# An attention and two-layer gated network kernel: the first unit's steps in another order, and the third unit's preparation later

## The chip, the cores and the metric

The kernel runs on one core of one Trainium2 chip. The metric is the device time of one execution in microseconds (us), from repeated runs; a profile is one more execution, with every instruction recorded.

## The reference, cut to what matters

Attention has two parts that are added: one over q, k, v averaged in groups of 4 positions (its result is repeated 4 times), and a local one in which a position sees those less than 4 away. Two gated layers of matrix products follow, over 2304 tokens of 512 features, with 2048 hidden features, all in float32.

```python
q_d = q.reshape(B, H, Sd, 4, D).mean(axis=3)          # k_d, v_d alike
out_up = np.repeat(sm_attn(q_d, k_d, v_d), 4, axis=2)
mask = np.abs(pos[:, None] - pos[None, :]) < 4
...
out = out_up + np.matmul(attn, v)                     # attn: softmax of the masked scores
h = x @ w_in;  x2 = (h * sigmoid(h)) @ w_out          # first layer (moe)
h = x2 @ w_in2; y = (h * clip(h + 3, 0, 6) / 6) @ w_out2   # second layer (moe2)
```

The four batches have 8 heads, 576 positions and 64 values per head; the inputs are drawn at random, and the weights come as 64-bit floats.

## The kernel before, in words

**Units and passes.** The 2304 tokens are cut into 8 units of 288 (half a batch); the work of a unit is its attention and then its first layer. The first layer runs over f = 0 to 15, slices of 128 hidden features. An iteration is one f of one unit: 12 matmuls `h<-xhl,w` (`gemm1`), the gate (`t` on ACT by a tanh, then on DVE), the split of the gated value into a high part `gh` (ACT) and a low part `gl` (POOL), and, up to two iterations later, 12 matmuls `y` (`y_unit1`). Every operand is split in a high and a low part, so that three products of the fast format make one of float32; `xhl` is such a pair of an input x. The order of the passes is: the first pass is unit 0 with f 0 to 7; the second is unit 1 with all 16; the third is unit 0 with f 8 to 15; then units 2 to 7 follow, and the second layer after them in blocks of 512 tokens.

**Weights.** The 32 weight tiles of a layer (`order` numbers them 0 to 31 as they are needed) are loaded as 64-bit words (`raw`, 512 KB each) and converted: ACT takes the upper words (`wu`), POOL or ACT the exponent bytes (`wt`), DVE joins them in two instructions (`wt<-wu,wt`), ACT rounds to the high part (`w<-wt`), and POOL subtracts for the low part (`w<-wt,w`). `step` does one such conversion; the first pass and the second have one or two steps in each iteration.

**The first unit's attention** stands in the list `PROLOGUE`, written out by hand. Its names: `turns` (k and q turned by matmuls `nt` with their sums), `ds` (averaged scores), `ls` (local scores), `sums` (v summed by fours on POOL: `vraw`, then `vd`), `dx` (maximum `dm` and exponential `de` of averaged scores), `dn` (normalized by `dr`), `dt` (transposed), `dv` (averaged values `od`), `le`, `ln`, `lt`, `lp` (local exponential, normalization, transposition to `leT`, and spreading into `pT`, a part of the tile `xo`), `lv` (local values, with `od` added: x of the unit), `warm` (n dummy matmuls `idle`), `keep_x` (x of unit 0 stored for the third pass). Every call is held behind what each engine was given last.

**Later units.** The attention of unit 1 is spread over the first pass, that of unit 2 over the second and third by `attention`: two places per iteration, 48 in all for unit 2. Before it comes the preparation: for each of 4 pairs of heads the loads of q and k into `qkraw` (a tile of two buffers, which `vraw` shares) and their transposes and sums on DVE (`xe<-qkraw`, `xe<-xe`, `xo<-xe`), then 8 loads and sums of v (`vd<-vraw`). In unit 2 they start at place 0, and the attention's steps at place 21.

**Order.** What is written is a program order; a scheduler then merges the engines' queues with regard to dependences and its own estimate of times, and may draw a load ahead where nothing holds it. Each engine, and SP's queue of loads, works strictly in the order of its own queue; a TensorE weight load may run ahead.

## Time and profile before

| | |
|---|---|
| median of 3 runs | 981.69 us (980.3 to 983.03) |
| the profiled execution | 980.93 us, of which 979.1 us lie between its first and last instruction |
| TensorE busy with matmuls | 944.3 us, 96% of the span |
| DVE, ACT, POOL busy | 46%, 40%, 26% of the span |
| mean granted clock of TensorE | 0.986 of full speed |

The time is read as a sum of stages: what TensorE does and where it waits. Busy shares over the whole span say little about the first 200 us, in which other engines have far more work than later.

### The profile page before, as it was taken

To read this page: it belongs to the slowest core of one execution; us is meant where nothing else is said; L and a number is where in the kernel's file an instruction comes from. 1 tells how busy PE (TensorE), PEld (TensorE's weight loads), DVE (VectorE), ACT (ScalarE), POOL (GpSimd) and SP (SyncE) were. 2 spreads that over 40 slices of the span, in tenths; PEclk is the share of its full clock that TensorE was granted. 3 is DMA by queue.
4 is the path that set the end of the run, shared out by engine and by line. 5 is a ranking of instruction groups with operands and counts; after the bars stand their busy time and mean duration, and the time that the engine had idled before them with its cause. 6 is when DMAs were issued, how large, how long until landed. Compare 5 with 4: busy or idle time off the path is not lost.

```text
span 979.1 us, 18978 instructions
## 1 busy us (share of the span) xinstructions
PE 944.3 (96%) x7654; PEld 829.4 (85%) x7654; DVE 448.4 (46%) x911; ACT 388.8 (40%) x894; POOL 257.9 (26%) x326
## 2 busy tenths in 40 slices
PE   8789797999999999999999999999999999999998
PEld 5677787999999989999999988888888888888897
DVE  4787588148361384432515878422223222322222
ACT  4576355324333342343425676333224222322232
POOL 6387484213222122132222688200000000000000
PEclk9789999999999999999999999999999999999999
DMA  7958722231231123101007960001002000100010
GB/s 188 328 122 247 210 59 36 75 65 41 69 63 23 49 49 69 39 7 52 2 1 255 370 218 1 1 22 65 0 1 74 13 1 1 43 1 1 1 44 22
DMA packets 125855, 71.68 MB, mean 73 GB/s; under 512 B 86088, under 2 KB 119112, under 8 KB 125768
## 3 DMA queue, kind: packets, MB, share of 16 engines
q1 hardware_dynamic: 121160, 65.76, 24.3%
q10 hardware_dynamic: 4608, 4.72, 1.4%
q8 instruction: 60, 0.98, 0.4%
q14 instruction: 27, 0.22, 0.1%
HBM read 59.83 MB, written 10.62 MB: 72 GB/s over the span
## 4 chain that ended last, share of the span: by engine, by line
PE 78%; DVE 8%; DMA 6%; SPq 2%; issue 2%; ACT 2%; POOL 1%; ACTq 0%; DVEq 0%; POOLq 0%
PE h L612 36%; PE y L749 21%; PE y L719 15%; DMA qkraw<-in_q_dram 2%; SPq L212 2%; DVE wt L31 2%; DMA x2raw<-x2d 2%; PE lv L203 1%; PE ls L203 1%; PE dv L203 1%; DMA xo<-in_v_dram 1%; DVE xe L31 1%; DVE le L31 1%; PE dt L206 1%; DMA nat<-in_q_dram 1%
## 5 line engine op out<-in xcount | busy, mean ns | idle before, releaser
L612 PE MATMUL h<-xhl,w 128*128 128x288 f32 (+2 forms) x2496 | 447.6, 327 | 9.5 <-DVE wt L31 4.5
L612 PEld LDWEIGHTS h<-xhl,w 128*128 128x128 f32 x2496 | 380.3, 189 | 50.6 <-ACT xhl L31 4.5
L719 PE MATMUL y<-gh,w 128*128 128x288 f32 x1024 | 233.0, 303 | 7.0 <-ACT w L31 5.1
L31 DVE SCALAR_TENSOR_TENSOR t<-t,h 128x288 f32<-128x288 f32 (+2 forms) x208 | 107.7, 519 | 273.8 <-ACT t L31 273.8
L749 PE MATMUL y<-w,g 128*128 128x512 f32 x864 | 214.8, 395 | 0.0
L749 PEld LDWEIGHTS y<-w,g 128*128 128x128 f32 x864 | 161.3, 188 | 37.5
L719 PEld LDWEIGHTS y<-gh,w 128*128 128x128 f32 x1024 | 172.8, 190 | 12.4 <-ACT w L31 5.4
L31 POOL TENSOR_TENSOR gl<-t,gh 128x288 fp32r<-128x288 f32 x112 | 90.9, 812 | 260.3 <-ACT gh L31 257.5
L719 PE MATMUL y<-gl,w 128*128 128x288 f32 x512 | 150.4, 302 | 1.8 <-DVE gl L31 1.4
L31 DVE TENSOR_TENSOR g<-t,g 128x512 fp32r<-128x512 f32 (+1 forms) x80 | 55.2, 689 | 124.4 <-ACT g L31 124.4
L31 ACT ACTIVATE t<-h,three 128x512 f32<-128x512 f32 (+1 forms) x80 | 51.7, 647 | 140.0 <-PE h L612 139.7
L719 PEld LDWEIGHTS y<-gl,w 128*128 128x128 f32 x512 | 97.2, 190 | 4.7 <-DVE gl L31 2.6
L31 POOL TENSOR_TENSOR w<-wt,w 128x512 fp32r<-128x512 f32 x64 | 84.1, 1318 | 46.4 <-ACT w L31 40.8
L31 DVE SCALAR_TENSOR_TENSOR wt<-wu,wt 128x512 uint32<-128x512 uint32 x128 | 85.6, 683 | 22.8 <-ACT wu L31 14.5
L31 ACT CAST gh<-t 128x288 fp32r<-128x288 f32 x128 | 55.0, 431 | 102.7 <-PE y L719 64.1
L31 ACT ACTIVATE t<-h 128x288 f32<-128x288 f32 x128 | 51.9, 407 | 107.1 <-PE h L612 104.5
L31 ACT CAST g<-t 128x512 fp32r<-128x512 f32 (+1 forms) x80 | 46.3, 579 | 119.5 <-PE y L749 118.8
L31 ACT CAST w<-wt 128x512 fp32r<-128x512 f32 x64 | 39.6, 620 | 28.6 <-DVE wt L31 24.2
L31 POOL TENSOR_SCALAR wt<-raw 128x512 uint32<-128x512 uint8 x61 | 42.2, 692 | 12.2 <-DMA raw<-in_moe_w_in_dram 5.8
L31 ACT ACTIVATE wu<-raw 128x512 f32<-128x512 f32 x64 | 40.2, 636 | 1.6 <-DVE t L31 0.9
L31 DVE STREAM_TRANSPOSE xe<-qkraw 128x288 f32<-128x288 f32 (+1 forms) x36 | 19.8, 566 | 27.3 <-DMA qkraw<-in_q_dram 12.0
L31 POOL TENSOR_TENSOR de<-de,dr 72x288 f32<-72x288 f32 x30 | 20.4, 683 | 34.0 <-DVE dr L31 27.9
(71 smaller groups left out, 572.9 us busy)
## 6 DMA issues: line engine op xcount, KB each, us to landing
raw<-in_moe_w_in_dram SPq DMA_DIRECT2D x32, 512.0 KB
raw<-in_moe_w_out_dram SPq DMA_DIRECT2D x32, 512.0 KB
xo<-in_v_dram SPq DMA_DIRECT2D x88, 64.0 KB
vraw<-in_v_dram SPq DMA_DIRECT2D x32, 144.0 KB
x2d<-yo ACTq DMA_DIRECT2D x32, 144.0 KB
x2raw<-x2d SPq DMA_DIRECT2D x9, 512.0 KB
out_dram<-yo SPq DMA_DIRECT2D x18, 256.0 KB
qkraw<-in_q_dram SPq DMA_DIRECT2D x96, 36.0 KB
```

The source lines that it names most:

```text
L31: r = getattr(self.engine, name)(*args, **kwargs)
L203: latest[0] = nc.tensor.matmul(*args, **kwargs).ins
L206: latest[0] = nc.tensor.transpose(*args).ins
L212: nc.sync.dma_start(raw[64 * h + 32 * e:64 * h + 32 * e + 32], src[h, t0:t0 + n, 32 * e:32 * e + 32].rearrange("(n t) d -> t n d", t=32),)
L612: nc.tensor.matmul(o, w[:, hw, c, :], x[:, hx, c, :], start=(i == 0), stop=(i == 3 * NC - 1))
L719: nc.tensor.matmul(ys[m], w[:, hw, m * P:(m + 1) * P], r, start=(f == fs[0] and i == 0), stop=(f == fs[-1] and i == 2),)
L749: nc.tensor.matmul(y, l[:, m * P:(m + 1) * P], w[:, hw, :], start=(f == 0 and i == 0), stop=(f == NF - 1 and i == 2),)
```

## The change

It does six things. (1) `ds` of both pairs of heads comes before the local scores, and the averaged softmax is done up to its transposes before the local one begins; its normalization is on POOL for all heads, the local subtraction on DVE for both halves. (2) The first weight tile is loaded ahead of v; the tiles 0 and 1 are converted and split inside the prologue (before, one conversion, one split and a second conversion stood ahead of `lv`), in the two halves `conv_parts` and `conv_join`; in the tiles 0, 7, 9, 11, 13 and 15 ACT does the bytes (before: the tiles 9, 12 and 17). (3) x of unit 0 is added from PSUM straight into its SBUF tile, and split from there by `split_x0`; before, it was added in PSUM and then both split and copied. (4) Of the four late query turns (q of unit 1), two stand in the prologue; their loads come after the weight tile 3 instead of after tile 9. (5) The three product groups of `gemm1` go hi-hi, lo-hi, hi-lo, where the low part of the weight came last. (6) In unit 2 the preparation starts at place 10 instead of 0 (its first load at place 9, held there by a memset, and each later load one step ahead of its use), and the attention's steps at place 25 instead of 21, in 20 places instead of 22.

```diff
@@ -163,20 +163,29 @@
+        conv_parts(layer, part, f)
+        conv_join(layer, part, f)
+    def conv_parts(layer, part, f):
         raw = raws[layer, part, f]
         words = raw.rearrange("p (d w) -> p d w", w=2)
         up = words[:, :, 1]
-        early = layer == 0 and order.index((part, f)) < 5
+        i = order.index((part, f)) if layer == 0 else NF
+        early = i < EARLY
         ps = (ps_y if early else ps_w).tile([P, 512], F32, tag="y" if early else "w", name="wu")
         act.activation(ps[:, :DM], up.bitcast(F32), AF.Copy, scale=2.0 ** -112)
         t = pool.tile([P, DM], U32, tag="wt", name="wt", bufs=3)
         b = raw.bitcast(U8).rearrange("p (d w) -> p d w", w=8)[:, :, 3]
-        if layer == 0 and not early and f < 8 and f % 4 == 3:
+        if i == 0 or EARLY < i < NF and i % 2:
             act.activation(t, b, AF.Copy, scale=2.0 ** -5, bias=-31.0 / 64)
         else:
             gps.tensor_scalar(out=t, in0=b, scalar1=2.0 ** -5, scalar2=-31.0 / 64, op0=ALU.mult, op1=ALU.add)
-        u = ps[:, :DM].bitcast(U32)
+        raws[layer, part, f] = t, ps[:, :DM].bitcast(U32)
+    def conv_join(layer, part, f):
+        t, u = raws[layer, part, f]
         vec.scalar_tensor_tensor(
             out=t, in0=u, scalar=0x80000000, in1=t, op0=ALU.bitwise_and, op1=ALU.bitwise_or
         )
@@ -224,6 +233,8 @@
     def load_qk(u, c):
         b, hf = divmod(u, 2)
         raw = pool.tile([P, (S + UT) // 32, 32], F32, tag="stg", name="qkraw", bufs=2)
+        if u == 2:
+            gps.memset(raw[:, 0:1, 0:1], 0.0)
         load_heads(raw[:, S // 32:], q[b, 2 * c:2 * c + 2], hf * UT, UT)
         if hf == 0:
             load_heads(raw[:, :S // 32], k[b, 2 * c:2 * c + 2], 0, S)
@@ -304,8 +315,9 @@
     def down_scores(u, ch):
         ss = []
+        own = u == 0 and ch == 1
         for par in range(2):
-            ps = ps_w.tile([P, 512], F32, tag="w", name="ds")
+            ps = (ps_y if own else ps_w).tile([P, 512], F32, tag="y" if own else "w", name="ds")
@@ -376,7 +388,7 @@
...
-        if u == 0:
+        if u == 0 and c == 1:
             keep_warm(idle["ps"], 1, latest[0], 448)
     def local_exp(eng, u, s):
...
-    def local_spread(par, t, a):
+    def local_spread(par, t, a, turning=False):
         rows = slice(32 * a, 32 * a + 32)
-        copy = act.copy if a % 2 else vec.tensor_copy
+        copy = act.copy if a % 2 or turning else vec.tensor_copy
         copy(pT[rows, par * NC * G:(par + 1) * NC * G, QB * a:QB * (a + 1)], t[rows, :, 0:QB])
     def local_values(u, g, od, x):
@@ -425,19 +437,21 @@
                     pT[:, (par * NC + c) * G + g, 0:n], start=True, stop=True,
                 )
         s = ps[:, :NC * n].rearrange("p (c t) -> p c t", c=NC)
-        o = s if u == 0 else x[:, :, g * n:(g + 1) * n]
+        o = x[:, :, g * n:(g + 1) * n]
         vec.tensor_tensor(
             out=o.rearrange("p c (i r) -> p c i r", r=FACTOR),
             in0=s.rearrange("p c (i r) -> p c i r", r=FACTOR),
             in1=od[:, :, g * nd:(g + 1) * nd].unsqueeze(3).to_broadcast([P, NC, nd, FACTOR]),
             op=ALU.add,
         )
-        if u == 0:
-            hi, lo = x[:, 0, :, g * n:(g + 1) * n], x[:, 1, :, g * n:(g + 1) * n]
-            act.copy(hi, s)
-            vec.tensor_tensor(out=lo, in0=s, in1=hi.bitcast(F32), op=ALU.subtract)
-            act.copy(xs[0][:, :, g * n:(g + 1) * n], s)
+    def split_x0(g):
+        n = 4 * QB
+        s = xs[0][:, :, g * n:(g + 1) * n]
+        hi, lo = (xhl[0][:, i, :, g * n:(g + 1) * n] for i in range(2))
+        act.copy(hi, s)
+        vec.tensor_tensor(out=lo, in0=s, in1=hi.bitcast(F32), op=ALU.subtract)
     xs = {}
     NPOS = 2 * NF
@@ -445,14 +459,14 @@
     def attention_calls(u):
         st = {}
-        local_engines = ((vec, gps), (gps, gps), (vec, vec))[min(u, 2)]
-        down_engines = (gps if u else vec, gps)
+        local_engines = ((vec, vec), (gps, gps), (vec, vec))[min(u, 2)]
+        down_engines = (gps, gps)
         def begin():
             st["od"] = pool.tile([P, NC, UD], F32, tag="od", name="od", bufs=1)
             if u == 0:
-                xhl[0] = st["x"] = pool.tile([P, 2, NC, UT], F32R, tag="xhl", name="xhl", bufs=1)
-                xs[0] = pool.tile([P, NC, UT], F32, tag="x32", name="x32", bufs=1)
+                xhl[0] = pool.tile([P, 2, NC, UT], F32R, tag="xhl", name="xhl", bufs=1)
+                xs[0] = st["x"] = pool.tile([P, NC, UT], F32, tag="x32", name="x32", bufs=1)
         def ds(ch): st["ds", 2 * ch], st["ds", 2 * ch + 1] = down_scores(u, ch)
         def dx(i): st["e", i] = down_exp(u, i, st["ds", i])
@@ -463,7 +477,7 @@
         def le(i): st["le", i] = local_exp(local_engines[i], u, st["ls"][i])
         def ln(i): local_norm(local_engines[i] if u else vec, st["le", i])
         def lt(i): st["leT", i] = local_transpose(u, st["le", i])
-        def lp(i, a): local_spread(i, st["leT", i], a)
+        def lp(i, a): local_spread(i, st["leT", i], a, u == 0 and i == 0)
         def lv(g):
             if u and g == 0:
                 xs[u] = st["x"] = pool.tile([P, NC, UT], F32, tag="x32", name="x32", bufs=1)
@@ -491,8 +505,14 @@
                     prep += [[(load_vd, (u // 2, h)), (prep_vd, (u // 2, h))]]
             else:
                 prep = [[(load_qk, (u, i)), (prep_q, (i,))] for i in range(NC)]
+            if u == 2:
+                loads = [calls[0] for calls in prep] + [None]
+                prep = [[loads[i + 1]] * (i + 1 < len(prep)) + calls[1:] for i, calls in enumerate(prep)]
+                places[9].append((held, loads[:1]))
+            start = 10 if u == 2 else 0
             for i, calls in enumerate(prep):
-                places[i * first // len(prep)].append((held, calls))
+                places[start + i * (first - start) // len(prep)].append((held, calls))
             for i in range(4 * G):
                 places[i * first // (4 * G)].append((load_vw, (u, i // 4, i % 4)))
         return places
@@ -530,14 +550,16 @@
         22: [("lv", 2)],
     }
+    EARLY = 5
     PROLOGUE = [
-        ("turns", 0), ("turns", 1), ("begin",), ("ds", 0), ("ls", 0), ("ls", 1), ("ls", 2), ("ls", 3), ("ds", 1), ("warm", 14), ("sums",),
-        ("dx", 0), ("dx", 1), ("le", 0), ("dx", 2), ("dx", 3), ("le", 1),
-        ("dn", 0), ("dt", 0), ("warm", 3), ("dn", 1), ("dt", 1), ("warm", 8), ("ln", 0), ("lt", 0), ("dv", 0),
-        ("dn", 2), ("dt", 2), ("warm", 3), ("dn", 3), ("dt", 3), ("warm", 8),
-        ("lp", 0, 0), ("lp", 0, 1), ("lp", 0, 2), ("lp", 0, 3), ("dv", 1), ("warm", 4), ("ln", 1), ("lt", 1),
-        ("lp", 1, 0), ("lp", 1, 1), ("lp", 1, 2), ("lp", 1, 3), ("step",), ("step",),
-        ("lv", 0), ("lv", 1), ("lv", 2), ("warm", 12), ("keep_x",), ("step",), ("step",), ("step",),
+        ("turns", 0), ("turns", 1), ("begin",), ("ds", 0), ("ds", 1), ("ls", 0), ("ls", 1), ("ls", 2), ("ls", 3),
+        ("sums", 0), ("dx", 0), ("dx", 1), ("parts", 0), ("dx", 2), ("dx", 3), ("dn", 0), ("dn", 1), ("join", 0),
+        ("warm", 10), ("dt", 0), ("dt", 1), ("sums", 1), ("le", 0), ("warm", 4), ("dv", 0), ("warm", 14), ("parts", 1), ("le", 1),
+        ("dn", 2), ("dn", 3), ("split", 0), ("dt", 2), ("dt", 3), ("warm", 5), ("dv", 1), ("warm", 20),
+        ("ln", 0), ("lt", 0), ("lp", 0, 0), ("lp", 0, 1), ("lp", 0, 2), ("lp", 0, 3),
+        ("ln", 1), ("lt", 1), ("lp", 1, 0), ("lp", 1, 1), ("lp", 1, 2), ("lp", 1, 3), ("join", 1),
+        ("lv", 0), ("lv", 1), ("lv", 2), ("xs", 0), ("split", 1), ("xs", 1), ("xs", 2), ("step",),
+        ("late", 0), ("late", 1), ("keep_x",), ("step",),
     ]
@@ -607,7 +629,7 @@
         w = wi[layer, f]
         o = hp[:, :n]
         i = 0
-        for hw, hx in ((0, 0), (0, 1), (1, 0)):
+        for hw, hx in ((0, 0), (1, 0), (0, 1)):
             for c in range(NC):
                 nc.tensor.matmul(o, w[:, hw, c, :], x[:, hx, c, :], start=(i == 0), stop=(i == 3 * NC - 1))
                 i += 1
@@ -668,20 +690,21 @@
         for j in range(2):
             kn[i, j] = load_nat(k, 0, 4 * i, j)
         qn[i] = load_nat(q, 0, 4 * i, 0)
+    load_w(0, *order[0])
     for h in range(H):
         load_vd(0, h)
     for i in range(4 * G):
         if i % 4 == 0:
-            load_w(0, *order[i // 4])
+            load_w(0, *order[1 + i // 4])
         load_vw(0, i // 4, i % 4)
-    for o in order[3:10]:
+    qn1 = [load_nat(q, 0, 4 * i, 1) for i in range(2)]
+    for o in order[4:10]:
         load_w(0, *o)
-    qn1 = [load_nat(q, 0, 4 * i, 1) for i in range(2)]
     for o in order[10:16]:
         load_w(0, *o)
     idle["ps"] = ps_y.tile([P, 512], F32, tag="y", name="idle")
     keep_warm(idle["ps"], 10)
-    add_w([(0, *o) for o in order])
+    add_w([(0, *o) for o in order[2:]])
     def turns(i):
         for c in (2 * i, 2 * i + 1):
@@ -693,15 +716,23 @@
     def warm(n):
         keep_warm(idle["ps"], n, latest[0], 224)
-    def sums():
-        for h in range(H):
+    def sums(i):
+        for h in range(4 * i, 4 * i + 4):
             prep_vd(0, h)
+    def late(c):
+        turn_q(c, qn1[c // 2])
+    def split(i):
+        split_w(0, *order[i])
+        done.add((0, *order[i]))
     names = attention_calls(0)
     def keep_x():
         nc.sync.dma_start(x0d, xs[0])
-    names.update(turns=turns, warm=warm, sums=sums, step=step, keep_x=keep_x)
+    names.update(turns=turns, warm=warm, sums=sums, step=step, keep_x=keep_x, late=late, split=split, xs=split_x0)
+    names.update(parts=lambda i: conv_parts(0, *order[i]), join=lambda i: conv_join(0, *order[i]))
     for name, *args in PROLOGUE:
         with behind(dict(last)):
             names[name](*args)
@@ -779,10 +810,10 @@
     HF = NF // 2
     passes = [(0, range(HF)), (1, range(NF)), (0, range(HF, NF))] + [(u, range(NF)) for u in range(2, NU)]
     first_att = attention(1, 2 * HF, lambda p: 1 + p * 12 // 22)
-    for c in range(NC):
+    for c in range(2, NC):
         first_att[0].insert(0, (late_q, (c, qn1[c // 2])))
     first_att[0].sort(key=lambda call: call[0] is not late_q)
-    second_att = attention(2, 3 * NF, lambda p: 21 + p)
+    second_att = attention(2, 3 * NF, lambda p: 25 + p * 20 // 22)
     nxts = [first_att, second_att[:2 * NF], second_att[2 * NF:]]
     nxts += [attention(u, NPOS, lambda p: 6 + p) for u in range(3, NU)] + [[[] for _ in range(NPOS)]]
     x0 = [None]
```

**DVE, first unit.** DVE's queue in the prologue, from the second averaged maximum on. Before:

```order
L31 TENSOR_REDUCE dm<-ds 72x2
L31 TENSOR_SCALAR dm<-dm 72x2
L31 TENSOR_TENSOR le<-ls,mask 128x384
L31 TENSOR_REDUCE lm<-le 128x12
L31 TENSOR_TENSOR le<-le,lm 128x384
L31 TENSOR_REDUCE dm<-ds 72x2
L31 TENSOR_SCALAR dm<-dm 72x2
L31 TENSOR_REDUCE dm<-ds 72x2
L31 TENSOR_SCALAR dm<-dm 72x2
L31 TENSOR_TENSOR le<-ls,mask 128x384
L31 TENSOR_REDUCE lm<-le 128x12
L31 TENSOR_SCALAR dr<-dr 72x2
```

After:

```order
L31 TENSOR_REDUCE dm<-ds 72x2
L31 TENSOR_SCALAR dm<-dm 72x2
L31 TENSOR_SCALAR dr<-dr 72x2
L31 RECIPROCAL dr<-dr 72x2
L31 TENSOR_SCALAR dr<-dr 72x2
L31 RECIPROCAL dr<-dr 72x2
L31 SCALAR_TENSOR_TENSOR wt<-wu,wt 128x512 x2
L31 TENSOR_TENSOR le<-ls,mask 128x384
L31 TENSOR_REDUCE lm<-le 128x12
L31 TENSOR_TENSOR le<-le,lm 128x384
L31 TENSOR_TENSOR le<-ls,mask 128x384
L31 TENSOR_REDUCE lm<-le 128x12
```

The first local half stood between the two pairs of averaged heads; now all averaged maxima and the first two sums `dr` stand ahead, with the join of weight tile 0, and the two local halves behind each other.

**PE, the first products.** PE's queue around the first `h` of the kernel (L612 before is L634 after, L203 is L212, L582 is L604, L719 is L750). Before:

```order
L582 MATMUL idle<-zeros 128x224
L612 MATMUL h<-xhl,w 128x288 x4
L203 MATMUL nt<-ident,nat 64x72 x13
L612 MATMUL h<-xhl,w 128x288 x8
L203 MATMUL nt<-ident,nat 64x72 x19
L719 MATMUL y<-gh,w 128x288 x4
L719 MATMUL y<-gl,w 128x288
```

After:

```order
L604 MATMUL idle<-zeros 128x224
L212 MATMUL lv<-xo 64x96 x3
L212 MATMUL nt<-ident,nat 64x72 x8
L212 MATMUL lv<-xo 64x96 x21
L212 MATMUL nt<-ident,nat 64x72 x8
L634 MATMUL h<-xhl,w 128x288 x8
L212 MATMUL nt<-ident,nat 64x72 x10
L634 MATMUL h<-xhl,w 128x288 x4
L212 MATMUL nt<-ident,nat 64x72 x6
L212 MATMUL ls<-xe 32x32 x86
L634 MATMUL h<-xhl,w 128x288 x12
```

Eight of the twelve products stand in one run now, since they need no low part of x; half of the late query turns `nt` lie ahead of them, and 12 dummy matmuls between `lv` and `h` are gone.

**DVE, second pass.** DVE's queue from the low parts of unit 1's x on. Before:

```order
L31 SCALAR_TENSOR_TENSOR wt<-wu,wt 128x512
L31 SCALAR_TENSOR_TENSOR t<-t,h 128x288 x2
L31 STREAM_TRANSPOSE xe<-qkraw 128x576
L31 STREAM_TRANSPOSE xe<-qkraw 128x288
L31 STREAM_TRANSPOSE xe<-qkraw 128x576
L31 STREAM_TRANSPOSE xe<-qkraw 128x288
L31 TENSOR_REDUCE xe<-xe 128x144
L31 TENSOR_REDUCE xo<-xe 128x72
L31 SCALAR_TENSOR_TENSOR wt<-wu,wt 128x512
L31 TENSOR_REDUCE xe<-xe 128x144
L31 TENSOR_REDUCE xo<-xe 128x72
L31 SCALAR_TENSOR_TENSOR t<-t,h 128x288 x2
```

After:

```order
L31 SCALAR_TENSOR_TENSOR wt<-wu,wt 128x512
L31 SCALAR_TENSOR_TENSOR t<-t,h 128x288 x2
L31 SCALAR_TENSOR_TENSOR wt<-wu,wt 128x512
L31 SCALAR_TENSOR_TENSOR t<-t,h 128x288
L31 SCALAR_TENSOR_TENSOR wt<-wu,wt 128x512 x2
L31 SCALAR_TENSOR_TENSOR t<-t,h 128x288
L31 SCALAR_TENSOR_TENSOR wt<-wu,wt 128x512 x2
L31 SCALAR_TENSOR_TENSOR t<-t,h 128x288
L31 SCALAR_TENSOR_TENSOR wt<-wu,wt 128x512 x3
L31 SCALAR_TENSOR_TENSOR t<-t,h 128x288
L31 SCALAR_TENSOR_TENSOR wt<-wu,wt 128x512 x2
L31 SCALAR_TENSOR_TENSOR t<-t,h 128x288
L31 STREAM_TRANSPOSE xe<-qkraw 128x288
```

Before, four transposes of unit 2 stand behind the gates `t` of the last iteration of the first pass and the first of the second, and ahead of three joins; now the first stands behind the gate of the sixth iteration.

## Rows read from the trace of the kernel before

**Rows 1.** Busy time by stage (PE, PEld, DVE, ACT, POOL), then clock, DMA share, GB/s

```profile
43.30:89.80 46.50, 42.53 (x544) 37.86 (x545) 35.49 (x76) 34.32 (x82) 37.41 (x53) 0.89 0.74 205
89.80:167.40 77.60, 63.30 (x607) 59.00 (x605) 62.36 (x123) 38.47 (x94) 44.81 (x52) 0.96 0.50 117
167.40:198.70 31.30, 31.30 (x284) 29.69 (x283) 7.12 (x18) 11.99 (x34) 7.70 (x11) 1.00 0.23 60
198.70:979.10 780.40, 773.62 (x5661) 678.48 (x5660) 318.38 (x637) 283.13 (x636) 145.16 (x165) 1.00 0.18 52
```

**Rows 2.** Chain of waits: start, length (us), what

```profile
259.47 3.19 PE y L719 x24
```

**Rows 3.** Timeline of all engines, first unit: start, length, engine, line, operation, [wait]

```profile
12.15 1.42 POOL L31 TENSOR_TENSOR vraw<-vraw 72x256 f32<-72x256 f32 x2 [3.59 <-DMA vraw<-in_v_dram]
...
29.44 1.35 POOL L31 TENSOR_TENSOR de<-de,dr 72x288 f32<-72x288 f32 x2 [3.60 <-DVE dr L31]
```

**Rows 4.** The same, end of the first unit's averaged values, added x, first gate

```profile
34.41 0.28 ACT L31 COPY od<-dv 128x144 f32<-128x144 f32 x1 [0.99 <-PE dv L203]
...
39.01 0.56 DVE L31 TENSOR_TENSOR lv<-lv,od 128x384 f32<-128x384 f32 x1
...
48.18 0.41 ACT L31 ACTIVATE t<-h 128x288 f32<-128x288 f32 x1 [0.56 <-PE h L612]
```

**Rows 5.** Timeline of PE around the first products

```profile
35.62 2.19 PE L203 MATMUL lv<-xo 128*64 128x96 f32 x42 [0.16 <-ACT xo L31]
...
43.28 0.79 PE L612 MATMUL h<-xhl,w 128*128 128x288 f32 x4 [4.20 <-ACT xhl L31]
...
45.85 2.29 PE L612 MATMUL h<-xhl,w 128*128 128x288 f32 x8
```

**Rows 6.** Groups of instructions, whole run: busy us, mean ns of one, waits before

```profile
L31 POOL TENSOR_SCALAR wt<-raw 128x512 uint32<-128x512 uint8 x61 | 42.2, 692 | 12.2 <-DMA raw<-in_moe_w_in_dram 5.8 <-DMA x2d<-yo 1.4
...
L31 ACT COPY xo<-leT 32x288 f32<-32x288 f32 x32 | 13.7, 430 | 7.9 <-DVE dr L31 4.1 <-DVE leT L31 3.4
...
L31 POOL TENSOR_TENSOR vd<-vraw 72x128 f32<-72x128 f32 x8 | 3.4, 452 | 0.0
...
L31 ACT ACTIVATE wt<-raw 128x512 uint32<-128x512 uint8 x3 | 2.0, 669 | 0.0
```

**Rows 7.** Stretch of 10 to 15 us, columns as in rows 1

```profile
10.00:15.00 5.00, 4.93 (x111) 3.91 (x114) 3.42 (x9) 4.33 (x8) 2.36 (x4) 1.00 0.90 244
```

**Rows 8.** Groups of DVE from 89.8 to 167.4 us, columns as in rows 6

```profile
L31 DVE SCALAR_TENSOR_TENSOR wt<-wu,wt 128x512 uint32<-128x512 uint32 x32 | 21.5, 679 | 2.0 <-POOL wt L31 1.8
L31 DVE TENSOR_REDUCE vd<-vraw 72x128 f32<-72x512 f32 x8 | 8.6, 1089 | 0.7 <-DMA vraw<-in_v_dram 0.7
L31 DVE SCALAR_TENSOR_TENSOR t<-t,h 128x288 f32<-128x288 f32 x17 | 7.4, 440 | 0.6 <-ACT t L31 0.6
...
L31 DVE STREAM_TRANSPOSE xe<-qkraw 128x288 f32<-128x288 f32 x8 | 3.7, 460 | 10.6 <-DMA qkraw<-in_q_dram 10.6
...
L31 DVE STREAM_TRANSPOSE xe<-qkraw 128x576 f32<-128x576 f32 x4 | 3.0, 762 | 1.2 <-DMA qkraw<-in_k_dram 1.2
...
L31 DVE TENSOR_TENSOR le<-le,lr 128x384 f32<-128x384 f32 x2 | 2.4, 1250 | 0.0
```

**Rows 9.** Timeline of DVE in the second pass

```profile
110.42 0.48 DVE L31 STREAM_TRANSPOSE xe<-qkraw 128x288 f32<-128x288 f32 x1 [8.59 <-DMA qkraw<-in_q_dram]
```

**Rows 10.** Timeline of PE: two waits of the second pass

```profile
101.94 0.51 PE L719 MATMUL y<-gh,w 128*128 128x288 f32 x1 [5.13 <-ACT w L31]
...
160.26 3.25 PE L612 MATMUL h<-xhl,w 128*128 128x288 f32 x12 [2.05 <-DVE wt L31]
```

**Rows 11.** Stretches behind these two waits, columns as in rows 1

```profile
103.00:105.00 2.00, 2.00 (x10) 1.87 (x9) 0.00 (x0) 0.60 (x3) 0.25 (x1) 0.50 1.06 376
...
160.00:164.00 4.00, 3.74 (x17) 3.75 (x18) 3.96 (x12) 1.81 (x5) 2.89 (x4) 0.57 0.00 0
```

**Rows 12.** Chain of waits: a load of unit 2's preparation

```profile
113.22 3.29 DMA qkraw<-in_k_dram
```

## The prediction, made before the changed kernel was run

> **What bounds the kernel now.** I read the busy time by stage first. From 198.7 us on TensorE (PE) works 773.6 of 780.4 us, nothing of the change lies there, and so all that can be won or lost lies ahead of it [rows 1]. In the three passes before, the reader should compare each engine with the length. In the third pass PE is busy for the whole 31.3 us. In the first pass it is busy 42.5 of 46.5 us, and no other engine is near the length. In the second pass it works 63.3 of 77.6 us, part of that at the lower clock, while DVE works 62.4: there the two hinder each other. An iteration (12 `h` and 12 `y`) needs about 3.19 us of PE, by the 24 products of one link in the chain of waits [rows 2], so the 24 iterations of second and third pass need 76.6 us, and they take 108.9.
>
> Then the timeline of the first 50 us: PE begins its first `h` at 43.28, after 4.20 us of waiting for the high part of x, and only at 48.18 the first gate starts [rows 4, 5]. What stands ahead is a chain: v arrives, POOL sums it from 12.15 on, and normalizes the last exponentials `de` until 30.79 [rows 3]; ACT has `od` at 34.69 [rows 4].
>
> Last the second pass by DVE's groups and its timeline: it idles 15.2 us, of which 10.6 and 1.2 are waits for the loads of q and k [rows 8], 8.59 in one place [rows 9]. Weight joins `wt` stand behind these in DVE's queue, and PE waits 5.13 us for a weight [rows 10].
>
> **The change, part by part.** *First unit.* The first weight's load, now ahead of v, is 0.5 MB; at the 244 GB/s of that stretch [rows 7] it delays v by 2.1 us, and POOL starts at 14.3. Its new queue is four heads at 0.71 + 0.45 us (4.6 us, to 18.9), two `de` (1.35, to 20.3), four heads (to 24.9), one `wt` of 0.69 (to 25.6), two `de` (to 27.0) [rows 3, 6]. With 0.5 us for waits between (my choice) that is 27.5. Before, `od` was there 3.9 us after this point (34.69 − 30.79) [rows 3, 4]; with and without two of ACT's spreading copies of 0.43 us [rows 6] in between that makes 30.5 to 31.4, and I take 31.0. All of the first half's spreading is now ACT's: six copies, 2.6 us, to 33.6. The local values start at about 34.0, or at 35 if the 20 dummies ahead run at 1.2 GHz. The 48 `lv` with 8 late turns between them take 2.5 + 0.6 us by the 2.19 us of 42 [rows 5], to 37.1. The last addition of 0.56 us [rows 4] and a rounding of nearly the same size on ACT bring the first `h` to 38.2 instead of 43.28. The additions no longer wait for each other's split, since they go to SBUF. Eight `h` (0.79 for four [rows 5]) need no low part of x, four more follow behind ten turns; ACT has three `wu`, two `xe` and one `w` ahead of the gate, some 3.9 us, so the gate starts at 42.1 instead of 48.2. **Gain 6.0**, from 4.5 (dummies at the low clock, more waits) to 7.5 (no waits, ACT's queue shorter).
>
> *First pass.* Two of four late turns are already done, and ACT does the bytes of three more tiles, 0.67 us each, which POOL is spared (0.69 each) [rows 6]. ACT then has about 34.3 + 2.0 less two turns' copies, POOL 37.4 − 2.1, in 46.5 us [rows 1]: neither becomes the bound, but neither was the only one either, since the conversions of two tiles per iteration pass in turn through ACT, POOL, DVE and ACT. I take the length as **unchanged**, ±2.
>
> *Second pass.* Unit 2's preparation leaves the first five iterations. There DVE has only two joins (0.68 each) and a gate (0.44) [rows 8], 1.8 us in an iteration of 3.2: it idles 1.4 us in each, over six iterations 8 us, but PE is never kept waiting. At the end some 5 us of DVE's attention work, such as the two normalizations of 1.25 us [rows 8] with their transposes and copies, falls behind the pass. The loads are now held until place 9, behind all weight loads; in before the last of k took 3.29 us with little beside it [rows 12]. Each is issued one step ahead of its use, so I set 2.5 us of waits for all four pairs, between nothing and the 8.59 of one wait [rows 9]. DVE's pass then lasts 62.4 − 5 + 8 + 2.5 = 67.9 instead of 77.6 us: **gain 9.7**, bounds 12 (no waits) and 4 (the 5 us stay, or a wait as long as now).
>
> A stretch of this pass gets denser, though. From f = 5 to 12 DVE has 17 joins (11.5 us), 8 gates (3.5), the transposes of four pairs (4.8), as much again (an estimate) for their reductions, and 8 sums of v (8.6) [rows 8]: 33 us in eight iterations, 4.1 each, where PE needs 3.2. PE then waits about 0.9 us in every iteration. What its clock does there is open. Behind the wait of 5.13 us the granted clock was 0.50, the 1.2 GHz level, and around the one of 2.05 it was 0.57 [rows 10, 11], where 12 products took 3.25 us against half of 3.19 [rows 2]. No row shows waits of under 1 us one behind the other lowering it, so I put nothing into the sum. The Trainium skill ("TensorE: Matmul & The Clock Gate", section "HAM oscillation — how this bites in real kernels") speaks against this change: it says that gaps that come back in every turn of a loop keep returning the clock to its low level, each burst starting cold. By the rule the dense stretch would go at the low clock again and again, which is the third rival below; the two rows agree as to single long waits.
>
> *Third pass.* Unit 2's attention starts two iterations later and ends one later, at place 45 of 48. Between its last values and its first `h` the addition (0.56), four roundings and four subtractions must fit into the last iteration's rest and two groups of `y` (about 1.6 + 3.2 us) [rows 2, 4]. DVE is busy 7.1 of 31.3 us here, ACT 12.0 [rows 1], so the 5 us from above and this are nearly covered; PE would show what isn't. **Loss 1.5**, from 0 to 3.
>
> *Product order.* The same 12 products; no cost. The low part of w, now needed four products earlier, is done by POOL well ahead except in f = 0.
>
> Sum: 6.0 + 0 + 9.7 − 1.5 = 14.2 us. The profiled execution took 980.93 us, 0.76 below the median of 981.69. So the profile would show about 966.7, and the median 967.5. A difference of 0.3% (2.9 us) is about what a measurement can tell from none.
>
> **The rivals.**
> 1. *Both gains, as worked out*: 967.5, by the bounds of the terms 958 to 973. For it: the waits of both places are seen in the profile. Chance 0.62.
> 2. *The first unit's gain is given back in the first pass*, because conversions set its pace and not the start of the products: weight tiles arrive no earlier (the loads run at 244 GB/s already at 10 to 15 us [rows 7]) and their conversion on ACT and POOL begins when the prologue releases them. Against it: ACT and POOL idle 12.2 and 9.1 of 46.5 us [rows 1]. 981.69 − 9.7 + 1.5 = 973.5. Chance 0.12.
> 3. *PE's clock falls in the dense stretch.* At 1.2 GHz an iteration takes 6.4 us instead of DVE's 4.1; if four of the eight run so, that costs 4 × 2.3 = 9 us: 976.5. Against it: waits of 0.9 us are less than the 2.05 after which it was seen. Chance 0.11.
> 4. *2 and 3 together*: 982.5, no difference. Also here if the preparation's waits eat what the first unit gives. Chance 0.06.
> 5. *Slower: DVE is blocked by the later loads.* Each pair's loads are now issued only when a buffer and its memset on POOL come free, and DVE's queue has joins behind each transpose. If each of four pairs waits as the one of 8.59 us does now [rows 9], the pass takes 62.4 − 5 + 8 + 34.4 = 99.8, 22 more than now: 981.69 − 6.0 + 22.2 + 1.5 = 999.5. It decides when all these waits exceed 2.5 + 14.2 = 16.7 us, two such waits. Against it: the long wait fell into a stretch where weights were still loading, and the load of k later took 3.29 [rows 12]. Chance 0.09.
>
> **How the numbers follow.** The likeliest case gives 967.5. To hold 8 in 10, the range takes in the first three cases, from 957 to 977. The first three are faster (0.85 in all), the fourth is within 0.3%, 0.06, and the last slower, 0.09.
>
> **What would show it.** In the changed kernel's timeline: the first `h` near 38 and the first gate near 42 us; POOL's last `de` of the first unit by 27.5. If the first pass still ends near 89.8 although it began 6 earlier, rival 2 holds; it should end near 84. In the second pass PE no longer waits some 5 us for a `w` near its start, DVE waits less than 2 us for any `qkraw`, and the granted clock between f = 5 and 12 stays above 0.9; a value near 0.6 is rival 3, waits of 8 us for `qkraw` are rival 5. The third pass should begin at 151 to 153 and unit 2's products at about 184 to 185, with PE waiting under 3 us for x there. Later rows should not move but by this shift. The prediction would be wrong above all if an engine that I take as covered, ACT in the prologue or POOL with its memsets, turns out to stand ahead of a join.

## The result, and the profile after

The change took the median from 982.36 to 972.12 us (4 runs each; those of the changed kernel lie between 969.37 and 973.22). A fourth run of the kernel before, 985.68, is why its median is no longer 981.69. The ratio is 0.9888, with a 95% interval of 0.9852 to 0.9925: faster. The gain is 10.2 us where 14.2 were forecast, and the time lies in the range of 957 to 977, 4.6 above the 967.5. The profiled execution took 973.22 us, 971.4 of them between first and last instruction, 7.7 less than before. Where they came from is read from the busy time by stage of the changed kernel, cut at the first `h` of each pass (columns as in [rows 1]):

```profile
43.92:90.39 46.47, 39.57 (x504) 35.51 (x504) 38.25 (x78) 33.41 (x81) 34.69 (x50) 0.85 0.60 175
90.39:157.26 66.87, 60.39 (x597) 56.17 (x597) 52.34 (x93) 34.37 (x78) 46.78 (x57) 1.00 0.57 144
157.26:191.84 34.58, 34.31 (x299) 31.35 (x297) 15.89 (x49) 16.61 (x53) 9.74 (x12) 1.00 0.37 80
191.84:971.40 779.56, 772.09 (x5662) 678.16 (x5660) 318.35 (x637) 282.99 (x636) 145.71 (x165) 1.00 0.18 52
```

Cut in the same way, the kernel before has its first `h` at 43.28, the second pass at 89.83, the third at 167.38 and unit 2 at 198.66. So the first unit lost 0.6 us where the forecast had it win 5.1 at the first `h` (and 6.0 at the first gate); the first pass kept its length (46.5 and 46.5); the second became 10.7 shorter (66.9 against 77.6, 67.9 forecast) and the third 3.3 longer (34.6 against 31.3); the rest gained 0.9. That sums to 7.7.

The first unit is where forecast and profile part. The timeline of the changed kernel, engine by engine (start, length, then the wait in brackets):

```profile
5.04 0.72 PE L212 MATMUL nt<-ident,nat 72*64 72x72 f32 x16
6.38 0.72 PE L212 MATMUL nt<-ident,nat 72*64 72x72 f32 x16 [0.62 <-DMA nat<-in_k_dram]
8.00 1.23 PE L212 MATMUL nt<-ident,nat 72*64 72x72 f32 x16 [0.90 <-DMA nat<-in_q_dram]
...
9.65 3.15 PE L212 MATMUL nt<-ident,nat 72*64 72x72 f32 x48
...
14.83 1.42 POOL L31 TENSOR_TENSOR vraw<-vraw 72x256 f32<-72x256 f32 x2 [6.00 <-DMA vraw<-in_v_dram]
...
25.68 1.29 POOL L31 TENSOR_TENSOR de<-de,dr 72x288 f32<-72x288 f32 x2 [5.73 <-DVE dr L31]
...
43.92 1.33 PE L634 MATMUL h<-xhl,w 128*128 128x288 f32 x8 [0.79 <-ACT xhl L31]
...
48.63 0.40 ACT L31 ACTIVATE t<-h 128x288 f32<-128x288 f32 x1
```

and its windows there (columns as above):

```profile
6.00:8.00 2.00, 0.72 (x16) 0.57 (x16) 0.61 (x2) 1.14 (x2) 1.68 (x6) 0.96 1.08 240
8.00:26.00 18.00, 18.00 (x337) 14.21 (x340) 7.83 (x24) 10.36 (x27) 5.54 (x12) 0.50 0.90 212
```

v is summed from 14.83 on, near the forecast 14.3, and the two `de` were expected at 18.9; but POOL waits 5.73 us for their `dr`, since the averaged scores are late. They are late because PE waited 0.62 and 0.90 us for loads of k and q, and then ran from 8 to 26 us at a granted clock of 0.50, the 1.2 GHz level: 48 turns take 3.15 us. In the kernel before the first 48 turns run in one piece, the window from 6 to 8 us has PE at work for 1.99 of 2.00 us, and the clock stays up (48 turns take 1.72 us):

```profile
5.57 2.38 PE L203 MATMUL nt<-ident,nat 72*64 72x72 f32 x48
7.88 0.36 PE L582 MATMUL idle<-zeros 128*128 128x448 bf16 x1
8.17 1.72 PE L203 MATMUL nt<-ident,nat 72*64 72x72 f32 x48
```

```profile
6.00:8.00 2.00, 1.99 (x47) 1.74 (x43) 0.46 (x1) 1.22 (x3) 1.68 (x6) 1.00 0.83 211
8.00:20.00 12.00, 9.64 (x303) 7.52 (x302) 6.97 (x15) 7.73 (x18) 7.33 (x14) 1.00 0.87 213
```

### The profile page after: what moved, and what is told of

Same layout as the page of the kernel before. It is cut to its first block, busy times and chain, and to the rows that moved or that the text cites. A ratio compares the mean times of both kernels' runs of the same rounds, so it can differ in the third digit from the quotient of the medians.

```text
span 971.4 us, 18968 instructions
## 1 busy us (share of the span) xinstructions
PE 944.6 (97%) x7652; PEld 830.7 (86%) x7652; DVE 447.9 (46%) x908; ACT 389.2 (40%) x896; POOL 259.6 (27%) x328
## 4 chain that ended last, share of the span: by engine, by line
PE 80%; DVE 7%; DMA 4%; issue 2%; POOL 2%; ACT 2%; SPq 2%; ACTq 0%; DVEq 0%; POOLq 0%
PE h L634 36%; PE y L780 21%; PE y L750 16%; DMA x2raw<-x2d 2%; SPq L221 2%; PE lv L212 2%; DVE wt L31 1%; PE dv L212 1%; PE ls L212 1%; PE nt L212 1%; PE ds L212 1%; POOL w L31 1%; DVE dm L31 1%; DVE le L31 1%; POOL wt L31 1%
## 5 line engine op out<-in xcount | busy, mean ns | idle before, releaser
L634 PE MATMUL h<-xhl,w 128*128 128x288 f32 (+2 forms) x2496 | 448.3, 328 | 7.8 <-DVE t L31 3.1
L634 PEld LDWEIGHTS h<-xhl,w 128*128 128x128 f32 x2496 | 380.9, 189 | 49.3 <-DVE t L31 3.8
L750 PE MATMUL y<-gh,w 128*128 128x288 f32 x1024 | 230.9, 301 | 3.4 <-ACT gh L31 2.2
L750 PEld LDWEIGHTS y<-gh,w 128*128 128x128 f32 x1024 | 171.1, 189 | 8.9 <-ACT gh L31 3.1
L750 PE MATMUL y<-gl,w 128*128 128x288 f32 x512 | 150.4, 301 | 1.7 <-DVE gl L31 1.6
L750 PEld LDWEIGHTS y<-gl,w 128*128 128x128 f32 x512 | 96.9, 189 | 4.6 <-DVE gl L31 2.6
L31 POOL TENSOR_TENSOR de<-de,dr 72x288 f32<-72x288 f32 x32 | 22.4, 703 | 35.8 <-DVE dr L31 24.0
L31 DVE TENSOR_REDUCE vd<-vraw 72x128 f32<-72x512 f32 x24 | 25.4, 1075 | 8.8 <-DMA vraw<-in_v_dram 4.2
```

Source lines behind the costliest of these rows:

```text
L31: r = getattr(self.engine, name)(*args, **kwargs)
L634: nc.tensor.matmul(o, w[:, hw, c, :], x[:, hx, c, :], start=(i == 0), stop=(i == 3 * NC - 1))
L750: nc.tensor.matmul(ys[m], w[:, hw, m * P:(m + 1) * P], r, start=(f == fs[0] and i == 0), stop=(f == fs[-1] and i == 2),)
```

## The experiments

Theory at first: the weight's load, now ahead of v, delays k and q and so lowers the clock. Rivals: chance in one execution; or the clock is not what holds the first unit. Apart from this the runs try whether the third unit's later work alone gives the gain of the passes. The runs after the first two of the table were made in three groups (a_again to u2_late_only, fill to steps_23, before_fill to steps_27); each group has its own runs of the kernel before (medians 982.0 to 983.0), so that a ratio to those is safer than a difference of two medians from different groups. The stages in the one profile of each run (us; "waits" is what DVE waits for `qkraw` and `vraw` from 100 to 170 us), and the median of its runs:

| run | first `h` | first pass | second | third | waits | median (runs) |
|---|---|---|---|---|---|---|
| before | 43.28 | 46.55 | 77.55 | 31.28 | 12.5 | 982.36 (4) |
| after | 43.92 | 46.47 | 66.87 | 34.58 | 2.6 | 972.12 (4) |
| a_again | 43.81 | 46.43 | 69.58 | 34.61 | 4.2 | 969.46 (6) |
| w0_behind_v | 44.27 | 46.70 | 64.67 | 34.60 | 1.8 | 966.65 (6) |
| u2_as_before | 37.86 | 46.79 | 76.78 | 31.23 | 9.9 | 974.07 (7) |
| u2_late_only | 45.74 | 48.12 | 65.49 | 34.82 | 2.8 | 976.39 (12) |
| fill | 38.53 | 46.19 | 69.76 | 34.62 | 4.2 | 966.88 (5) |
| fill_w0_behind_v | 36.84 | 46.14 | 64.32 | 34.60 | 1.1 | 965.21 (5) |
| few_dummies | 43.36 | 46.25 | 64.32 | 34.60 | 1.7 | 969.49 (5) |
| steps_23 | 36.97 | 45.81 | 73.99 | 33.32 | 2.4 | 974.74 (9) |
| before_fill | 42.34 | 49.57 | 78.01 | 31.24 | 12.8 | 980.39 (12) |
| fill_old_products | 38.38 | 46.65 | 69.62 | 34.82 | 4.7 | 971.59 (6) |
| fill_late_as_before | 36.69 | 50.50 | 67.74 | 34.61 | 3.2 | 968.72 (6) |
| steps_27 | 39.02 | 45.92 | 66.24 | 34.72 | 2.7 | 968.28 (6) |

**a_again**, the changed kernel unaltered. 

> The changed kernel once more. Theory (the first weight's load, ahead of v, delays the loads of k and q, PE waits between its first turns, and its clock falls to 0.50 from 8 us on): the fall stands in this profile too, the granted clock of 10 to 20 us is about 0.50, the first h starts at 43 to 44 us, time 970 to 973 us. Rival (the fall was chance in one execution): clock 1.00 there, first h at about 38, time 966 to 968.

 The profile shows the fall again (first `h` at 43.81), but its execution took 975.06, the longest of six that begin at 967.77. So the fall is no accident of one execution, and yet the median, 969.46, lies between the two cases. A mean granted clock is on record for every execution: a fall from 8 to 26 us should lower it by about 18.00 × 0.5 / 971, or 0.009. Of the ten executions of the changed kernel five have 0.979 to 0.981 (969.77 to 975.06 us, median 973.2), both profiles among them, and five 0.985 to 0.989 (967.77 to 971.03, median 969.2). So about half of them seem to have the fall.

**w0_behind_v**

```diff
-    load_w(0, *order[0])
     for h in range(H):
         load_vd(0, h)
+    load_w(0, *order[0])
```

> The changed kernel with the first weight tile's load behind the eight loads of v, as it stood before; PE's queue is the same. Theory (load delays k and q): the 48 turns run in one piece, the clock of 10 to 20 us is 1.00, the averaged scores are done at 15 instead of 21 us, the first h starts at 37 to 39, and the time falls by about 5 to 966 to 968 us. Rival 1 (the clock falls for another reason, such as the order of the turns): clock 0.50 there, first h at 43 to 44, 970 to 973. Rival 2 (conversions set the first pass): first h at 38, but the second pass still begins at about 90, and the time stays at 970 to 973.

 The clock fell all the same (0.53 from 8 to 26 us), after PE had waited 0.20 and 0.80 us. The load's place is not the cause of the fall, and the first theory is dead.

```profile
6.38 0.72 PE L212 MATMUL nt<-ident,nat 72*64 72x72 f32 x16 [0.20 <-DMA nat<-in_k_dram]
7.90 0.72 PE L212 MATMUL nt<-ident,nat 72*64 72x72 f32 x16 [0.80 <-DMA nat<-in_q_dram]
```

```profile
8.00:26.00 18.00, 18.00 (x375) 14.32 (x376) 8.51 (x25) 10.83 (x28) 6.25 (x13) 0.53 0.96 221
```

The median is nevertheless 966.65. The profile is of the slowest of the six executions, 971.56: it and one more (970.24) have a mean clock of 0.980, the other four 0.989 to 0.991 and 964.90 to 967.26 us. The median is one of executions that seem not to have the fall.

**u2_as_before**: in the changed kernel, places 10 and 25 back to 0 and 21.

```diff
-            gps.memset(raw[:, 0:1, 0:1], 0.0)
...
-    second_att = attention(2, 3 * NF, lambda p: 25 + p * 20 // 22)
+    second_att = attention(2, 3 * NF, lambda p: 21 + p)
```

> The changed kernel with the third unit's preparation and attention at their old places (no memset, loads from place 0, steps from place 21). Theory (this part alone gives the gain, 10.7 us in the second pass less 3.3 in the third): the second pass lasts 76 to 79 us again, PE waits some 5 us for a weight near its start, time 979 to 981. Rival (the bytes of five more tiles on ACT, or the other turns' places, gave it): the second pass stays under 71 us, time 971 to 975.

 The second pass is back at 76.78, the third at 31.23, and PE waits 3.42 us for a weight near its start: the passes' gain is this part's. The time is under the expected one, 974.07 instead of 979 to 981, because the rest of the change has a gain of its own, and the profile shows where: in it the load still stands ahead of v, PE waited only once (0.62 us) among the first 48 turns, and the clock stayed at 1.00 until the averaged scores began:

```profile
7.58 0.72 PE L212 MATMUL nt<-ident,nat 72*64 72x72 f32 x16 [0.62 <-DMA nat<-in_q_dram]
```

```profile
6.00:8.00 2.00, 1.38 (x42) 1.23 (x40) 0.73 (x2) 1.18 (x2) 1.68 (x6) 1.00 1.04 249
8.00:16.00 8.00, 7.63 (x170) 6.16 (x166) 4.76 (x12) 6.05 (x10) 1.49 (x5) 1.00 0.85 224
```

The first `h` came at 37.86 and the first gate at 42.57, where 38.2 and 42.1 were forecast. With the load ahead of v the fall can be absent, and without it the fall can be there: the load is not the cause, though it may change how often the fall comes (five of ten against two of six by the mean clocks).

**u2_late_only**: the same part put into the kernel before. 

> The kernel before with only the third unit's preparation and attention later. Theory (this part alone gives the gain): second pass 66 to 69 us, third 34 to 35, time 974 to 976 us. Rival (it takes the rest of the change too): over 979. If the first unit's rest brought nothing at all, it equals the changed kernel, 972.

 Second and third pass are 65.49 and 34.82, as expected; the median is 976.39. The part works alone. By the ratios within its group it gives 5.8 us (0.9941), the rest of the change without it 6.4 (u2_as_before, 0.9935), and both together 11.8 (a_again, 0.9880): within the noise the two parts add up. In its profile the first `h` stands at 45.74, 2.5 us later than in the kernel before with the same code there; a single first `h` is no exact measure.

**fill**: the second theory, that PE's waits among its first turns lower the clock, tried by giving it work there.

```diff
                 turn_k(c, j, kn[i, j])
+                if c == 0:
+                    keep_warm(idle["ps"], 4, latest[0], 448)
```

> The changed kernel with four dummy products of 448 columns behind each of the first two turns of k, so that PE has work while it waits for the next load; nothing else moves. Theory (PE's waits between its first turns, 0.6 to 0.9 us each and of another size in each execution, let its clock fall at 8 us): granted clock 1.00 from 8 to 16 us, averaged scores begin at 15 to 16, first h at 37 to 39.5, second pass from 84 to 86; median 966 to 968.5 us, and the runs lie closer together than 967.8 to 975.1. Rival (the clock falls whatever PE does there): 0.50 from 8 on, first h at 43 to 45, median 969 to 973.

 PE's timeline, and the windows:

```profile
5.43 0.72 PE L212 MATMUL nt<-ident,nat 72*64 72x72 f32 x16
6.08 0.93 PE L604 MATMUL idle<-zeros 128*128 128x448 bf16 x4
6.94 0.72 PE L212 MATMUL nt<-ident,nat 72*64 72x72 f32 x16
7.59 0.93 PE L604 MATMUL idle<-zeros 128*128 128x448 bf16 x4
8.45 0.72 PE L212 MATMUL nt<-ident,nat 72*64 72x72 f32 x16
```

```profile
6.00:8.00 2.00, 2.00 (x29) 1.11 (x24) 0.46 (x1) 0.97 (x2) 1.67 (x6) 1.00 1.05 217
8.00:26.00 18.00, 16.16 (x428) 12.61 (x426) 13.57 (x32) 12.37 (x35) 10.84 (x20) 1.00 0.98 216
```

The clock is 1.00 from 8 to 26 us, the first `h` at 38.53, the first gate at 43.23. The median is 966.88 (964.09 to 968.88), against 970.4 over the ten executions of the changed kernel. The theory holds: eight dummies that do nothing give 3.5 us (3.6 to 4.4 by the ratios). One profile with the clock up would prove little, since u2_as_before has it without dummies; the mean clocks say more. Of the 28 executions of the changed kernel's five variants with dummies one is at 0.981 and the others are at 0.984 to 0.993, while 7 of the 16 of the changed kernel and w0_behind_v are at 0.979 to 0.981. Why the loads of k and q land so late in some executions that PE waits, stays open.

**fill_w0_behind_v**: both edits. 

> The same dummies, and the first weight tile's load behind those of v. If the place of the load has a price of its own (it delays v by 2 us, and the sums of v are on the way to the first unit's end): first h 1 to 2.5 us earlier than with the dummies alone, median 964 to 966. If it has none, because the averaged softmax is late and not v: the same within 1 us.

 The median is 965.21 (962.99 to 966.61), 0.9829 of the kernel before (0.9801 to 0.9858), the fastest of all. These are the numbers expected if the place has a price, and w0_behind_v also lies 2.8 us under a_again. But a price is not shown: the first `h` stands at 36.84 here and at 39.02 in steps_27, whose first unit is the same code, and the intervals overlap.

**few_dummies**

```diff
-    keep_warm(idle["ps"], 10)
+    keep_warm(idle["ps"], 5)
```

> The changed kernel with 5 instead of 10 dummy products at the start, so that PE is idle for 2 us more ahead of its first turns. Theory (waits there make the clock fall): the clock is 0.50 by 8 us in every execution, first h at 43 to 45, median 972 to 975. Rival (it has nothing to do with PE's idling): as the changed kernel, median 969 to 972, runs from 967 to 975.

 The first `h` is late as expected (43.36), and the turns run at the low level's pace. The median, 969.49, is that of the rival, and the theory's 972 to 975 was missed: the profiled second pass was short (64.32), so that a late first unit is not the whole of the time.

```profile
4.75 4.14 PE L212 MATMUL nt<-ident,nat 72*64 72x72 f32 x50 [1.24 <-DMA nat<-in_k_dram]
...
9.31 3.14 PE L212 MATMUL nt<-ident,nat 72*64 72x72 f32 x46
```

**steps_23**: steps of unit 2 from place 23 on.

```diff
-    second_att = attention(2, 3 * NF, lambda p: 25 + p * 20 // 22)
+    second_att = attention(2, 3 * NF, lambda p: 23 + p * 20 // 22)
```

> The changed kernel with the third unit's steps from place 23 instead of 25. Theory (the 3.3 us that the third pass got longer are products of unit 2's scores that went there from the second pass, no waits): third pass 32 to 33.5 us, second pass longer by as much, both together 101 to 104 as now, median within 2 us of the changed kernel's 969.5 to 972. Rival (unit 2's end is late and PE waits for it): both together 2 to 3 us shorter, median under 968.

 Both were wrong about the sum: second and third pass together take 107.3 us, 6 more than after, nearly what they took before (108.8). Only 1.3 of the third pass's 3.3 us came back, and the second pass lost most of its gain: PE waits 7.4 us there for three gates `t` from DVE. The preparation had two places less, too, as its end moves with the first step; that this made the waits is likely, not shown, for DVE's waits for loads did not grow (2.4).

**before_fill**: the dummies of fill in the kernel before. 

> The kernel before with the same eight dummies behind the first two turns of k. It tells how much of the change's gain is left when neither kernel's clock can fall at 8 us. Theory (the fall befalls the kernel before too, in part of its executions): clock 1.00 from 8 to 16 us, first h at 42 to 45, median 978 to 981 us instead of 982 to 983; the kernel with the change, the dummies and the load behind v then stands at a gain of 13 to 16 us against it. Rival (the kernel before was never touched by it): 982 to 984, the dummies cost what they last.

 The median is 980.39, a ratio of 0.9986 (0.9968 to 1.0004), which is no difference that can be told. Its first `h` came at 42.34, 0.9 earlier, and the profile lost that again in the first pass (49.57 instead of 46.55), where PE waits for the late queries, which are loaded behind more weights there:

```profile
42.34 0.80 PE L612 MATMUL h<-xhl,w 128*128 128x288 f32 x4 [4.21 <-ACT xhl L31]
46.28 1.91 PE L203 MATMUL nt<-ident,nat 72*64 72x72 f32 x26 [3.14 <-DMA nat<-in_q_dram]
```

With the same dummies in both, the change gives 980.4 − 966.9 = 13.5 us (14.0 by the ratios), where 14.2 were forecast, and with the load behind v as well 15.2. The kernel before may have the fall too: of its 17 executions in this group 7 have a mean clock of 0.973 to 0.977, with the dummies all twelve have 0.979 to 0.986. No profile shows one of the seven; that of the kernel before, at 0.986, is as high as the highest of the 17, so that the profiles before and after compare an execution without the fall with one that has it.

**fill_old_products**: in fill_w0_behind_v, `gemm1` again hi-hi, hi-lo, lo-hi.

```diff
-        for hw, hx in ((0, 0), (1, 0), (0, 1)):
+        for hw, hx in ((0, 0), (0, 1), (1, 0)):
```

> The changed kernel with the dummies and the load behind v (965.2 us), the product groups in their old order. Theory (the first gate, not the first product, sets what follows, and it waits for the low part of x in either order): first h still near 37, first gate 0 to 1 us later, median 964 to 967. Rival (eight products in one run are part of the first unit's gain): median 967 to 969.

 The median is 971.59 (967.45 to 974.62), 6.4 us more, or 5.2 by the ratios, and each of its runs is slower than every run of fill_w0_behind_v: the new order gains, where "no cost" put it at nothing. In the profile 1.5 us stand ahead of the first `h` and 5.3 in the second pass, where DVE waited 4.7 us for loads instead of 1.1. Whether the order makes these waits, or they fell together, one profile doesn't tell.

**fill_late_as_before**: in fill_w0_behind_v, all four late turns in the first pass.

```diff
-        ("late", 0), ("late", 1), ("keep_x",), ("step",),
+        ("keep_x",), ("step",),
...
-    for c in range(2, NC):
+    for c in range(NC):
```

> The same kernel with all four late turns of q in the first pass again. Theory (turns on PE in the shadow of the first x cost nothing, and the first pass does not get longer by them): first h at 36.2 to 37, first pass 46 to 47.5 us, median within 2 us of 965.2. Rival (they delay unit 1's scores and so the first pass): first pass 48 to 50, median 967 to 970.

 The first pass takes 50.50 us instead of 46.14, the median is 968.72: the rival. The turns ahead of the products are worth about 4 us of the pass; the ten profiles that have them there lie between 45.8 and 46.8.

**steps_27**: in fill_w0_behind_v, steps from place 27 on.

```diff
-    second_att = attention(2, 3 * NF, lambda p: 25 + p * 20 // 22)
+    second_att = attention(2, 3 * NF, lambda p: 27 + p * 18 // 22)
```

> The same kernel with the third unit's steps from place 27 in 18 places (last values at the same place). Moving them from 25 to 23 cost 5 us. Theory (DVE's dense stretch and its waits for the loads of v set the second pass's end): a longer preparation relieves it, second pass 61 to 64 us instead of 64.3, third pass 35 to 37, median 963 to 966. Rival (the steps bunch up in the third pass, unit 2 is late there): third pass 38 or more, median over 967.

 The second pass took 66.24, the third 34.72, the median is 968.28, 3.1 more: neither holds, and later than 25 brings nothing.

**DVE's waits and the second pass.** The column of waits orders the second pass in all nine profiles with places 10 and 25: 64.3 to 64.7 us with waits of 1.1 to 1.8; 65.5 to 66.9 with 2.6 to 2.8; 67.7 with 3.2; 69.6 to 69.8 with 4.2 to 4.7. That is an order, not a test: no run changed the waits alone. The longest waits of DVE for loads in three of them (line waited for, us in total, times, longest), fill_w0_behind_v, the changed kernel and a_again:

```profile
DVE vd L31 <- DMA vraw<-in_v_dram: 0.6, 1, 0.6
DVE xe L31 <- DMA qkraw<-in_q_dram: 0.3, 1, 0.3
```

```profile
DVE vd L31 <- DMA vraw<-in_v_dram: 1.2, 2, 0.9
DVE xe L31 <- DMA qkraw<-in_q_dram: 0.8, 2, 0.6
```

```profile
DVE vd L31 <- DMA vraw<-in_v_dram: 3.3, 2, 2.7
```

A gate `t` stands behind a sum of v in DVE's queue, and PE waits for that gate, 2.12 us in the changed kernel's profile, 4.15 in a_again's:

```profile
148.71 1.85 PE L634 MATMUL h<-xhl,w 128*128 128x288 f32 x12 [2.12 <-DVE t L31]
```

```profile
150.16 2.57 PE L634 MATMUL h<-xhl,w 128*128 128x288 f32 x12 [4.15 <-DVE t L31]
```

Two profiles of the same code, 66.87 and 69.58, differ by this above all. Behind the longer wait the twelve products take 2.57 us instead of 1.85, and the granted clock is 0.50 from 152 to 154 us.

## Why the prediction was right, and where it was not

The time lies in the range, and the change is faster by the two parts that the forecast named. But luck has a share in it. The range was wide, and "by the bounds of the terms 958 to 973" does not follow from the bounds: added up, they give 960.2 to 978.2. And some terms were wrong in opposite directions, as follows.

**First unit (6.0 forecast at the gate, −0.6 at the first `h` of the profile).** The failed step is the premise behind POOL's queue: all that stands ahead of v's sums, the first turns and the averaged scores, was taken to run as before. Nothing in the change touches it but the weight's load, and that is not the cause (w0_behind_v, u2_as_before). The end of the chain that I costed is right where the clock stays up: 37.86 and 38.53 for the first `h`, 42.57 and 43.23 for the first gate, against 38.2 and 42.1. That is a gain of 5.0 to 5.6 us at the gate, inside 4.5 to 7.5. A link in it was late all the same: POOL's last `de` ended at 29.5 and 28.8 us, not at 27.5, and the steps behind it were shorter than forecast. In the profiles with two waits among the first turns (the changed kernel, a_again, w0_behind_v) the gain is gone; with one, of 0.62, it stands (u2_as_before). The median of the changed kernel lies between.

**First pass (0 forecast, 0.1).** Right as a sum, wrong as a term: fill_late_as_before shows 4 us won by the late turns ahead, so that something of this size was lost in it as well. Against the profile before, PE has 3.0 us less work in the pass (39.57 instead of 42.58) and 2.9 us more idle time (6.90 instead of 3.97). The longest wait is for the exponentials of unit 1's averaged scores, and within the pass before no wait exceeds 0.97:

```profile
67.53 3.25 PE L634 MATMUL h<-xhl,w 128*128 128x288 f32 x12 [2.56 <-ACT de L31]
```

What makes it late stays open. Rival 2, that the pass gives the first unit's gain back, fell: with the first `h` at 37.86 the second pass began at 84.65.

**Second pass (9.7 forecast, 10.7).** The mechanism is right: PE's wait of 5.13 [rows 10] is gone, and DVE's waits for q and k fell from 11.8 to 1.4 us, where 2.5 were forecast (with those for v, from 12.5 to 2.6, and to between 1.1 and 4.7 over the runs). The sum is better than its terms. DVE's work fell by 10.0 us (62.4 to 52.3), where 5 were forecast, and it idles 14.5 us, where 8 + 2.5 were: two misses of 4 to 5 us that cancel. In the early iterations it idles because it waits for POOL, up to 3.15 us at a time:

```profile
L31 DVE SCALAR_TENSOR_TENSOR wt<-wu,wt 128x512 uint32<-128x512 uint32 x32 | 21.7, 681 | 9.9 <-POOL wt L31 9.8
```

Rival 5 (waits of 8 us each) fell. So did rival 3: the granted clock of the changed kernel's whole second pass is 1.00. Its condition hardly came about, for PE waited in the dense stretch not 0.9 us in every iteration but 1.01 and 0.79 in two, 11 and 12. What was held against it, that 0.9 is less than 2.05, is no safe reason: behind 0.20 and 0.80 us among the first turns the clock did fall (w0_behind_v). The rule of the Trainium skill ("TensorE: Matmul & The Clock Gate", section "HAM oscillation — how this bites in real kernels"), that gaps coming back in a loop keep the clock low, found no case in this pass. The loop that the Trainium skill describes there waits several times longer for its loads in each turn than PE does here, so that the prediction read more into the rule than it says. PE's waits for loads nearest to it are those of 0.62 and 0.90 us among the first turns, and I did not look there.

**Third pass (1.5 lost forecast, 3.3).** Mis-sized, and not for the reason given. PE is busy 34.31 of 34.58 us; unit 2 is not late. What came is work, 3.0 us more of it on PE, with half of the averaged scores and four more transposes than before:

```profile
L215 PE MATMUL dt<-ident,de 72*72 72x72 f32 x16 | 1.7, 227 | 0.3 <-POOL de L31 0.3
L212 PE MATMUL ds<-xe,xo 64*72 64x144 f32 x8 | 1.4, 297 | 0.0
```

The second pass got rid of the same products, so its gain is partly this shift. The two together gained 7.4 against the forecast 8.2, and that is waiting that is gone: PE is busy for 94.5 us in both passes before and 94.7 after, and idle for 14.3 and 6.8.

**Product order ("no cost").** Undoing it cost 5.2 to 6.4 us, so a gain of this size was left out of the sum; where it is made is not settled.

## What to carry to other kernels

A forecast that moves the end of a chain has to look at its head too: here PE waited there for several loads in turn, its clock fell in about half of the executions, as far as the mean clocks tell, and hid the gain, and eight dummy products in the waits kept it up. Where an engine has 15 us of idle time but the work comes in a lump behind late loads, move the lump to where its loads are in, and count products that cross a pass boundary as moved, not as won. A profile is one execution: here the same code gave second passes of 66.9 and 69.6 us, so set each term by several profiles before explaining a difference of 3 us, and look at the mean clock of every execution to see which kind the profile is.

## What was not expected of the hardware

Once at 1.2 GHz, PE stayed there from 8 to 26 us although it was busy for 18.00 of 18.00 us, with turns and scores.

In few_dummies the granted clock reads 1.00 from the start to 30 us, but 46 turns take 3.14 us, as 48 do at 0.50 in the changed kernel (3.15), and not 1.72 as at a true 1.00 in before:

```profile
8.00:26.00 18.00, 18.00 (x380) 14.60 (x377) 9.04 (x25) 10.76 (x29) 6.86 (x14) 1.00 0.90 217
```

The first change on its record is at 30 to 32 us (0.90, then 0.50); ahead of it the record does not tell the level, and a mean clock can miss a fall for the same reason. The Trainium skill ("TensorE: Matmul & The Clock Gate", section "Seeing it yourself") warns that trace events of this clock have been unreliable; this trace agrees, and the length of an instruction is the better witness.

DVE's `le<-le,lr` took 1250 ns each before [rows 8] and 600 after (0.54 and 0.66 us), at the same shape; after, both stand in the third pass instead of the second. What ran beside it was not tested.
